# Reordering the first batch of an attention + bilinear feed-forward kernel: transposes of a pair next to that pair's products, more dummy products, and a later identity

## Chip, cores, metric

The kernel runs on one core of a Trainium2 chip. The metric is the time of one execution in device microseconds.

In the text "dummies" are matrix products of zeros whose result nobody reads. They keep TensorE busy. The "granted clock" is the share of its full speed that TensorE had, as the profiler recorded it.

## The reference

```python
# attention part, per batch and head (8 x 8 heads, 576 tokens, head size 64)
kv  = einsum('bhsd,bhse->bhde', k, v)        # no softmax: 64x64 per head
out = einsum('bhsd,bhde->bhse', q, kv)
x   = out / sqrt(mean(out*out, -1) + 1e-6) * g_norm
# heads side by side: x is 4608 tokens x 512
# feed-forward: d_ff 1536
y   = ((x @ w_a) * (x @ w_b)) @ w_out
```

## The kernel before

TensorE does the work of the feed-forward strip by strip (9 strips of 512 tokens) and puts the attention of later batches between. Only the first batch has nothing to hide behind. It is done in four pairs of heads. For each pair:

- `early_qT(p)`: 12 transposes of q on TensorE, then one copy on VectorE out of PSUM, the memory that TensorE writes to.
- `early_kv(p)`: 12 small products k.T v, then two copies into a block-diagonal tile (ScalarE, then VectorE).
- `xu(p, h)`: x = q kv for half h of the tokens, and its square on ScalarE.
- `ss(p, h)`: sums of squares by a product with ones; then `norm`: reciprocal root on ScalarE, scaling on VectorE into `xt`, the input of the feed-forward.

Pair 0 is loaded in float32 by the hardware queues and cast on the engines. Pairs 1 to 3 are loaded with a cast by Pool's software queue, nine loads of 144 KB, and the weights follow in the same queue.

```python
for n, src, eng in (("q", q, nc.scalar), ("k", k, nc.sync), ("v", v, nc.sync)):
    ...                                        # raw loads of pair 0
ident = const.tile([128, 128], BF16)
make_identity(nc, ident)                       # on Pool, ahead of Pool's loads
for p in range(1, NP):                         # NP = 4
    early_load(early[0], 0, slice(2 * p, 2 * p + 2))   # q, k, v of pair p
# ... cut: weights, batch 1
dummies(10)
# ... casts of pair 0
at0.early_qT(0, fpsum)
at0.early_kv(0, fpsum)
dummies(3)
at0.xu(0, 0)
at0.xu(0, 1)
at0.early_qT(1, fpsum)
for p in range(1, NP):
    if p + 1 < NP:
        at0.early_qT(p + 1, fpsum)             # pair p+1 ahead of the products of pair p
    dummies(3)
    last = p == NP - 1
    at0.early_kv(p, fpsum, act=last)
    at0.ss(p - 1, 0, fpsum)
    if last:
        dummies(2)
    at0.xu(p, 0)
    # ... cut: ss(p - 1, 1), xu(p, 1)
# ... cut: last sums, then the feed-forward of strip 0 begins
```

Of the kernel before, what the change touches and what calls it, by code (L numbers as in the profile page):

```python
# [15 lines left out]
def kernel(  # L16
# [19 lines left out]
    NP = H // 2  # L36
# [21 lines left out]
    fpsum = ctx.enter_context(tc.tile_pool(name="fpsum", bufs=4, space=bass.MemoryType.PSUM))  # L58
# [20 lines left out]
    def early_tiles(b):  # L79
        t = {n: shared(n, H, EC)[0:EP] for n in ("k", "v")}  # L80
        t["q"] = first.tile([EP, H, EC, D], BF16, name=f"eq{b}")
        return t

    def early_load(t, b, hs):
        for n, src in (("q", q), ("k", k), ("v", v)):
            nc.gpsimd.dma_start(  # L86
                out=t[n][:, hs, :, :],
                in_=src[b, hs].rearrange("h (sp c) d -> sp h c d", c=EC),
            )

    early = [early_tiles(0), early_tiles(1)]
# [3 lines left out]
    for n, src, eng in (("q", q, nc.scalar), ("k", k, nc.sync), ("v", v, nc.sync)):  # L95
        raw[n] = first.tile([EP, 2, EC, D], FP32, name=f"raw_{n}")
        eng.dma_start(out=raw[n], in_=src[0, h0].rearrange("h (sp c) d -> sp h c d", c=EC))
    ident = const.tile([128, 128], BF16)
    make_identity(nc, ident)
    for p in range(1, NP):  # L100
        early_load(early[0], 0, slice(2 * p, 2 * p + 2))


# [71 lines left out]
    def dummies(n):  # L175
        if n:
            ps = apsum.tile([128, 512], FP32, name="w_ps", tag="at")
            for _ in range(n):
                nc.tensor.matmul(ps, lhsT=zt[:, 0:128], rhs=zt, start=True, stop=True)  # L179
# [210 lines left out]
    at0 = Attn(0, early[0])  # L390
# [3 lines left out]
    def lead(u, *kcs, pools=(None, None)):  # L394
        for kc in kcs:
            for which, pool in zip("ab", pools):
                us[u].mm(which, kc, pool)
# [9 lines left out]
    dummies(3)  # L407
    at0.xu(0, 0)
    at0.xu(0, 1)
    at0.early_qT(1, fpsum)  # L410
    for p in range(1, NP):
        if p + 1 < NP:
            at0.early_qT(p + 1, fpsum)
        dummies(3)
        last = p == NP - 1
        at0.early_kv(p, fpsum, act=last)
        at0.ss(p - 1, 0, fpsum)
        if last:
            dummies(2)
        at0.xu(p, 0)  # L420
        if not last:
            at0.ss(p - 1, 1, fpsum)
            at0.xu(p, 1)
    p = NP - 1
    at0.ss(p - 1, 1, fpsum, split=True)
    s21 = at0.s_ps
    at0.xu(p, 1)
    dummies(1)
    at0.ss(p, 0, fpsum)
    at0.norm(p - 1, 1, s21)  # L430
    at0.ss(p, 1, fpsum)
    lead(0, 0, 1, 2, pools=(fpsum, apsum))
    lead(1, 0, 1, 2)
    lead(0, 3)
# [103 lines left out]
```

## Time and profile before

| | before |
|---|---|
| median of the first three runs | 336.59 us |
| profiled execution | 336.12 us, span 334.2 us |
| TensorE busy | 97% of the span |
| first feed-forward product that needs xt of pair 2 | 24.70 us |

The page of the kernel before gives busy time by engine, and the granted TensorE clock in tenths of full speed in 40 slices of 8.36 us:

```profile
span 334.2 us, 4562 instructions
...
PE 324.5 (97%) x1761; PEld 155.2 (46%) x1761; DVE 131.0 (39%) x225; ACT 133.9 (40%) x280; POOL 62.2 (19%) x78
...
PEclk9769999999999999999999999999999999999999
```

TensorE is the bound. What can be gained is at the start, where it is busy with dummies or waits, and where the second and third slices show a clock of 0.7 and 0.6.

The timeline of TensorE before (start us, duration us, engine, line, what; in brackets the idle time ahead of it and what ended it):

```profile
8.18 0.56 PE L215 MATMUL q_ps<-ident,eq_91 96*64 96x96 bf16 x12
11.17 0.56 PE L215 MATMUL q_ps<-ident,eq_91 96*64 96x96 bf16 x12 [2.43 <-DMA eq_91<-in_q_dram]
11.66 0.82 PE L179 MATMUL w_ps<-zt 128*128 128x512 bf16 x3
12.41 0.67 PE L200 MATMUL kv_ps<-v_t,k_t 96*64 96x64 bf16 x12
...
15.26 1.46 PE L179 MATMUL w_ps<-zt 128*128 128x512 bf16 x3
16.65 0.66 PE L200 MATMUL kv_ps<-v_t,k_t 96*64 96x64 bf16 x12
...
20.18 0.66 PE L200 MATMUL kv_ps<-v_t,k_t 96*64 96x64 bf16 x12
...
24.70 0.38 PE L314 MATMUL a_ps<-xt_160,wa_t 128*128 128x512 bf16 x1 [0.23 <-DVE xt_160 L267]
```

The transposes at 8.18 are those of pair 1, those at 11.17 of pair 2. TensorE takes its products in the order of the program, so kv of pair 1 at 12.41 also waited for q of pair 2. By the semaphores of the trace all of pair 1 had landed at 10.39. Note the three dummies: 0.82 us at 11.66, but 1.46 us at 15.26.

The same stretch by windows (window, its length, busy time of each engine with instructions, PEclk, DMA share, GB/s):

```profile
8.96:12.37 3.41, 1.20 (x15) 0.64 (x15) 0.73 (x2) 0.00 (x0) 2.47 (x4) 1.00 1.31 199
12.37:22.61 10.24, 9.79 (x70) 4.65 (x70) 3.42 (x8) 4.75 (x14) 8.50 (x12) 0.50 1.54 190
```

In the first window TensorE was busy for 1.20 of 3.41 us. In the 10.24 us after it, it had half the clock, although it was busy.

One trap of these views: they count the time ahead of the first clock record (5.55 us in this profile) as full speed. The ten dummies at the start take 4.45 us, twice what ten take later (0.22 us from one to the next).

### The profile page before, as it was taken

The page shows a single profiled execution, that of the slowest core. Times are in us where ns is not written, and L with a number is a line of the kernel's source. Part 1 is how long each engine was busy: PE and PEld are TensorE (multiplying, and loading weights), DVE is VectorE, ACT ScalarE, POOL GpSimd, SP SyncE. Part 2 cuts the span into 40 slices and gives each one's busy share as a digit, 9 for nine tenths or more (in the row PEclk, how much of TensorE's full clock was granted, in tenths as well). Part 3 has the DMA queues.
Part 4 walks back from the last instruction along what each step waited for, and adds up shares of the span by engine and source line. Part 5 has one row for each costly group of instructions (what it writes and reads, how often), then busy time and mean ns, then how long its engine had stood idle before and what let it go on. Part 6 is the DMA issues. An engine that isn't in the chain of part 4 may idle for free.

```text
span 334.2 us, 4562 instructions
## 1 busy us (share of the span) xinstructions
PE 324.5 (97%) x1761; PEld 155.2 (46%) x1761; DVE 131.0 (39%) x225; ACT 133.9 (40%) x280; POOL 62.2 (19%) x78
## 2 busy tenths in 40 slices
PE   7699999999999999999999999999999999999995
PEld 3344454545544454444444454445444444444442
DVE  3334354455344433443345334524452333232311
ACT  3253364366355335632463336423553222323210
POOL 8865700703400610061004300000000000000000
PEclk9769999999999999999999999999999999999999
DMA  7999999995973793289215960410001010000022
GB/s 158 190 195 199 204 184 168 185 167 66 161 110 56 100 187 67 63 106 173 69 25 88 183 114 17 88 64 2 31 33 32 38 59 32 31 33 31 31 65 94
DMA packets 80230, 32.60 MB, mean 98 GB/s; under 512 B 51920, under 2 KB 75728, under 8 KB 80208
## 3 DMA queue, kind: packets, MB, share of 16 engines
q0 software_dynamic: 59888, 18.44, 50.9%
q1 hardware_dynamic: 19968, 13.44, 15.8%
q10 hardware_dynamic: 352, 0.43, 0.4%
q8 instruction: 14, 0.23, 0.3%
q14 instruction: 8, 0.07, 0.1%
HBM read 37.75 MB, written 12.98 MB: 152 GB/s over the span
## 4 chain that ended last, share of the span: by engine, by line
PE 94%; DMA 2%; ACT 1%; POOL 1%; DVE 1%; issue 0%; POOLq 0%; ACTq 0%
PE a_ps L314 28%; PE o_ps L342 28%; PE b_ps L314 28%; PE x_ps L243 3%; PE s_ps L258 3%; DMA eq_91<-in_q_dram 2%; PE kv_ps L231 2%; PE w_ps L179 1%; PE kv_ps L200 1%; PE q_ps L215 1%; ACT rs L265 1%; POOL eq_91 L86 0%; POOL k_t L86 0%; ACT qs_667 L221 0%; POOL v_t L86 0%
## 5 line engine op out<-in xcount | busy, mean ns | idle before, releaser
L326 DVE TENSOR_TENSOR abt<-b_ps,a_sb 128x512 bf16<-128x512 f32 x108 | 74.6, 692 | 119.1 <-PE b_ps L314 119.1
L324 ACT CAST a_sb<-a_ps 128x512 bf16<-128x512 f32 x108 | 63.1, 586 | 90.2 <-PE a_ps L314 88.4
L342 PE MATMUL o_ps<-wo_t,abt 128*128 128x512 bf16 x432 | 98.6, 379 | 0.0
L314 PEld LDWEIGHTS <-wb_t 128*128 128x128 bf16 x432 | 42.3, 98 | 51.3 <-issue 0.5
L342 PEld LDWEIGHTS <-abt 128*128 128x128 bf16 x432 | 42.3, 98 | 48.7 <-issue 0.5
L314 PEld LDWEIGHTS <-wa_t 128*128 128x128 bf16 x432 | 41.6, 98 | 43.1 <-DMA wa_t<-in_moe_w_a_dram 0.4
L314 PE MATMUL a_ps<-xt_160,wa_t 128*128 128x512 bf16 x108 | 40.9, 379 | 0.2 <-DVE xt_160 L267 0.2
L314 PE MATMUL a_ps<-xt_158,wa_t 128*128 128x512 bf16 x108 | 41.0, 380 | 0.0
L314 PE MATMUL a_ps<-xt_159,wa_t 128*128 128x512 bf16 x108 | 40.9, 379 | 0.0
L314 PE MATMUL b_ps<-xt_159,wb_t 128*128 128x512 bf16 x108 | 40.9, 379 | 0.0
L314 PE MATMUL a_ps<-xt_161,wa_t 128*128 128x512 bf16 x108 | 40.9, 379 | 0.0
L314 PE MATMUL b_ps<-xt_161,wb_t 128*128 128x512 bf16 x108 | 40.9, 379 | 0.0
L314 PE MATMUL b_ps<-xt_158,wb_t 128*128 128x512 bf16 x108 | 40.9, 379 | 0.0
L314 PE MATMUL b_ps<-xt_160,wb_t 128*128 128x512 bf16 x108 | 40.9, 379 | 0.0
L251 ACT ACTIVATE sq<-x_ps 128x288 bf16<-128x288 f32 x64 | 26.1, 410 | 29.7 <-PE x_ps L243 29.4
L265 ACT ACTIVATE rs<-s_ps,eps_t 128x288 f32<-128x288 f32 x64 | 31.5, 497 | 5.4 <-PE s_ps L258 4.9
L367 ACT COPY o_sb<-o_ps 128x512 f32<-128x512 f32 x17 | 9.9, 585 | 43.6 <-PE o_ps L342 43.6
L369 DVE COPY o_sb<-o_ps 128x512 f32<-128x512 f32 x18 | 12.4, 692 | 35.5 <-PE o_ps L342 35.5
L161 POOL COPY gate_t<-qT 1x1 bf16<-1x1 bf16 x5 | 0.9, 176 | 111.0 <-DMA qT<-scr 111.0
L148 POOL DMA_DIRECT2D scr<-in_q_dram x12 | 19.6, 1636 | 3.1 <-issue 2.4
L258 PE MATMUL s_ps<-sq,ones 128*128 128x288 bf16 x64 | 19.0, 300 | 0.6 <-ACT rs L265 0.4
L267 DVE SCALAR_TENSOR_TENSOR xt_160<-x_ps,g_col,rs 128x288 bf16<-128x288 f32 x16 | 8.3, 517 | 19.6 <-ACT rs L265 19.6
(76 smaller groups left out, 166.7 us busy)
## 6 DMA issues: line engine op xcount, KB each, us to landing
out_dram<-o_sb SPq DMA_DIRECT2D x23, 256.0 KB, 2.0
scr<-in_q_dram POOLq DMA_DIRECT2D x12, 288.0 KB, 6.7
k_t<-in_k_dram POOLq DMA_DIRECT2D x6, 512.0 KB, 8.7
v_t<-in_v_dram POOLq DMA_DIRECT2D x6, 512.0 KB, 10.8
out_dram<-o_sb SPq DMA_DIRECT2D x13, 128.0 KB, 2.4
wo_t<-in_moe_w_out_dram POOLq DMA_DIRECT2D x2, 768.0 KB, 14.8
wa_t<-in_moe_w_a_dram POOLq DMA_DIRECT2D x5, 256.0 KB, 8.6
wb_t<-in_moe_w_b_dram POOLq DMA_DIRECT2D x5, 256.0 KB, 9.2
```

Source lines behind the costliest of these rows:

```text
L148: nc.gpsimd.dma_start(out=scr[:, :, hl, :].rearrange("p s d -> s p d"), in_=qv[hl])
L243: nc.tensor.matmul(ps, lhsT=self.kvd[:, p, :], rhs=self.q[p][:, h * HF : (h + 1) * HF], start=True, stop=True,)
L251: nc.scalar.activation(sq, ps, AF.Square)
L258: nc.tensor.matmul(ps, lhsT=ones, rhs=self.sq[p, h], start=True, stop=True)
L265: nc.scalar.activation(rs, ps, AF.Abs_reciprocal_sqrt, bias=eps_t)
L267: nc.vector.scalar_tensor_tensor(out=xt[p][:, t0 : t0 + HF], in0=self.x_ps[p, h], scalar=g_col, in1=rs, op0=ALU.mult, op1=ALU.mult,)
L314: nc.tensor.matmul(getattr(self, which), lhsT=w[:, kc, self.fc * 128 : (self.fc + 1) * 128], rhs=xt[kc][:, t0 : t0 + STRIP], start=(kc == ...
L324: nc.scalar.copy(a_sb, self.a)
L326: nc.vector.tensor_mul(t, self.b, a_sb)
L342: nc.tensor.matmul(o_ps[s, g], lhsT=ab[s, fc][:, g * 128 : (g + 1) * 128], rhs=wo_t[:, fc, :], start=(fc == 0), stop=(fc == FC - 1),)
L367: nc.scalar.copy(o_sb, ps)
L369: nc.vector.tensor_copy(o_sb, ps)
```

## The change

The intent: let the transposes of a pair go directly ahead of that pair's own products, so that pair 1 doesn't wait for the loads of pair 2; fill the waits for loads with more dummies (6, 4, 4 for 3, 3, 3); and issue pair 1's loads ahead of the identity on Pool.

```diff
+    early_load(early[0], 0, slice(2, 4))
     ident = const.tile([128, 128], BF16)
     make_identity(nc, ident)
-    for p in range(1, NP):
+    for p in range(2, NP):
         early_load(early[0], 0, slice(2 * p, 2 * p + 2))
# ... cut
     at0.xu(0, 1)
-    at0.early_qT(1, fpsum)
+    last = NP - 1
     for p in range(1, NP):
-        if p + 1 < NP:
-            at0.early_qT(p + 1, fpsum)
-        dummies(3)
-        last = p == NP - 1
-        at0.early_kv(p, fpsum, act=last)
+        at0.early_qT(p, fpsum)
+        dummies(6 if p == 1 else 4)
+        at0.early_kv(p, fpsum, act=p == last)
         at0.ss(p - 1, 0, fpsum)
# ... cut: the rest of the loop is written differently, its order is the same
```

More of the change, by code (lines that the diff above doesn't have):

```diff
@@ L409 @@
     at0.xu(0, 1)
-    at0.early_qT(1, fpsum)
+    last = NP - 1
     for p in range(1, NP):
-        if p + 1 < NP:
-            at0.early_qT(p + 1, fpsum)
-        dummies(3)
-        last = p == NP - 1
-        at0.early_kv(p, fpsum, act=last)
+        at0.early_qT(p, fpsum)
+        dummies(6 if p == 1 else 4)
+        at0.early_kv(p, fpsum, act=p == last)
         at0.ss(p - 1, 0, fpsum)
-        if last:
+        if p == last:
             dummies(2)
         at0.xu(p, 0)
-        if not last:
-            at0.ss(p - 1, 1, fpsum)
-            at0.xu(p, 1)
-    p = NP - 1
-    at0.ss(p - 1, 1, fpsum, split=True)
-    s21 = at0.s_ps
-    at0.xu(p, 1)
+        at0.ss(p - 1, 1, fpsum, split=p == last)
+        at0.xu(p, 1)
+    s_ps = at0.s_ps
     dummies(1)
-    at0.ss(p, 0, fpsum)
-    at0.norm(p - 1, 1, s21)
-    at0.ss(p, 1, fpsum)
+    at0.ss(last, 0, fpsum)
+    at0.norm(last - 1, 1, s_ps)
+    at0.ss(last, 1, fpsum)
     lead(0, 0, 1, 2, pools=(fpsum, apsum))
```

## The prediction

> **What bounds it.** TensorE: the page gives PE 97% of the span, and the timeline shows it almost without gaps from 24.70 us, when the first feed-forward product on xt2 starts. The change touches only what is before, so its worth is how much earlier that point comes.
>
> The start, from the timeline and the semaphore times of the loads:
> - TensorE's order puts the transposes of pair 2 ahead of the products of pair 1. Pair 1 has landed at 10.39 (last is v), but TensorE waits idle from 8.74 to 11.17 for the q of pair 2 (the chain of waits: 7.6 us of that load), and kv of pair 1 runs only at 12.48.
> - The granted clock falls to 0.50 at 12.37 and stays there until 22.61, 10.24 us. The Trainium skill, "TensorE: Matmul & The Clock Gate", Part 1, puts the decision in free-running windows of 3413 ns; the trace agrees (10.24 = 3 x 3.413), and the window before the fall, 8.96 to 12.37, holds the idle 2.4 us. Under it a dummy product takes 0.43-0.48 us instead of 0.21.
> - Loads are a queue at about 0.7 us per 144 KB: q, k, v of pair 2 land at 11.12, 11.81, 12.55, of pair 3 at 13.35, 14.07, 14.77; the first four weight pieces at 15.5-17.7.
>
> **What changes.** Pool's identity (about 0.75 us ahead of the first load) moves behind pair 1's three loads; these are issued 0.75 us earlier, the later ones not. They then overlap the raw loads of pair 0, which may land 0-0.4 us later; I expect v of pair 1 at 9.7-10.3. Each pair becomes: transposes, dummies (6, then 4, 4), kv, sums and x. Five dummies more, 1.1 us warm, but they fill waits.
>
> **Sum (estimates from these durations, warm clock).** Transposes of pair 1 end at 8.8, six dummies at 10.1, kv of pair 1 at 10.2 (was 12.48). Copies 0.5 us, x: 11.3-11.7. Transposes of pair 2 to 12.3, dummies to 13.2, kv of pair 2 at 13.2 (was 16.72), x to 14.7; transposes 15.3, dummies 16.2, kv of pair 3 at 16.2 (was 20.2). The tail on ScalarE and VectorE (squares, reciprocal roots, xt2) 3.8 us, where it was 4.5: first xt2 product at about 20.0 instead of 24.70, 4.7 us earlier.
>
> **What of it lasts.** Weights land in time (piece for block 2 at 20.45, wanted at 22.5), batch 1's loads and wo too (43.65 against 46.0). Tightest is batch 2: its last v lands at 58.94, wanted at 64.4 now and 59.7 after; and the first three output writes (768 KB) would now run among those loads, not after them. I take off 0.3 us on average, up to 1.5.
>
> **Prediction:** 336.59 - 4.4 = 332.2 us, range 330.6 to 334.6; faster by over 2% 0.04, within 2% 0.94, slower 0.02.
>
> **Shows it right:** clock 1.0 from about 5.5 us to the end; no wait of TensorE for pair 2's q; kv of pair 1 at 10-10.6; first xt2 product at 19.5-20.5; everything from there shifted equally.
>
> **Shows it wrong:** clock still falling (the same page, Part 4, says transposes do not count as busy in the same way, so a window of transposes and small products may still count as idle): then about 2 us gained only. Raw loads of pair 0 late by over 0.5 us. TensorE waiting at batch 2's kv around 60 us for loads delayed by output writes: gain given back there.

## The result

The changed kernel took 332.63 us (median of four: 331.58, 331.84, 333.42, 333.50), before 336.60 (four runs, 336.28 to 336.74). The ratio is 0.988, 95% interval 0.984 to 0.992: clear of noise, and under 2%. Ratios here are the mean time of one kernel's fast runs over that of the other's in the same rounds, so not quite the ratio of the medians.

Two groups can be seen in the four times, about 1.8 us apart. They are called the slow and the quick group here. The first profile fell into the upper group (333.42 us). The same kernel was run again later, and that profile fell into the lower (331.44 us). Both are shown, since at the start they differ in one main thing, the time at which the clock rose.

The page of the second profile of the changed kernel:

```profile
span 329.5 us, 4572 instructions
...
PE 321.4 (98%) x1766; PEld 154.0 (47%) x1766; DVE 130.8 (40%) x225; ACT 134.1 (41%) x280; POOL 62.6 (19%) x78
...
PEclk9999999999999999999999999999999999999999
```

Its TensorE timeline, to be held against that of before:

```profile
8.13 0.56 PE L216 MATMUL q_ps<-ident,eq 96*64 96x96 bf16 x12
8.62 1.47 PE L180 MATMUL w_ps<-zt 128*128 128x512 bf16 x6
10.02 0.47 PE L201 MATMUL kv_ps<-v_t,k_t 96*64 96x64 bf16 x12
...
12.98 0.47 PE L201 MATMUL kv_ps<-v_t,k_t 96*64 96x64 bf16 x12
...
15.93 0.47 PE L201 MATMUL kv_ps<-v_t,k_t 96*64 96x64 bf16 x12
...
17.99 0.38 PE L180 MATMUL w_ps<-zt 128*128 128x512 bf16 x1 [0.54 <-DVE xt L268]
...
20.05 0.38 PE L315 MATMUL a_ps<-xt,wa_t 128*128 128x512 bf16 x1 [0.58 <-DVE xt L268]
```

No product waits for a load any more, and kv of the three pairs comes at 10.02, 12.98 and 15.93 instead of 12.41, 16.65 and 20.18. The first product on xt of pair 2 comes at 20.05 instead of 24.70: 4.65 us earlier. The span is 4.7 us shorter (334.2 - 329.5), so nothing was given back in this execution.

The windows that were shown of before:

```profile
8.96:12.37 3.41, 3.08 (x36) 1.59 (x34) 1.12 (x4) 1.70 (x5) 3.35 (x5) 1.00 1.31 200
12.37:22.61 10.24, 8.79 (x73) 4.21 (x71) 4.24 (x10) 5.17 (x15) 7.74 (x11) 1.00 1.55 191
```

TensorE is busy for 3.08 us of the first window, and the clock does not fall.

The first profile of the changed kernel, TensorE's timeline:

```profile
6.21 0.86 PE L216 MATMUL q_ps<-ident,eq 96*64 96x96 bf16 x12 [0.57 <-DVE eq L403]
...
7.41 1.46 PE L180 MATMUL w_ps<-zt 128*128 128x512 bf16 x3
...
10.08 1.70 PE L180 MATMUL w_ps<-zt 128*128 128x512 bf16 x6
11.71 0.47 PE L201 MATMUL kv_ps<-v_t,k_t 96*64 96x64 bf16 x12
...
21.74 0.38 PE L315 MATMUL a_ps<-xt,wa_t 128*128 128x512 bf16 x1 [0.58 <-DVE xt L268]
```

The three dummies at 7.41 take 1.46 us, the time of half the clock. Here the clock records begin at full speed only at 10.58 us; in the profile of before at 5.55, in the second one of the changed kernel at 5.84. Both start cold, at half speed, and this execution became warm 4.7 us later than the other. Neither the page nor the mean clock of an execution shows that: the mean is 1.0 for both. From there both go alike, 1.7 us apart (21.74 against 20.05), which is the distance of the two groups.

The clock records lie on a grid of 3.41 us (they last, for example, 6.83, 10.24 or 324.27 us, which is 2, 3 and 95 times 3.413) that has no fixed place against the start of the kernel. The Trainium skill, "TensorE: Matmul & The Clock Gate", Part 1, says so: the window "doesn't reset when your kernel starts". The two profiles agree. The window grid of the first puts a window at 3.76 to 7.17, into which the end of the ten dummies, 0.57 us of idle time and the first transposes fell; it did not raise the clock. The grid of the second puts one at 2.43 to 5.84, which is dummies to 94%; it did. In the other twelve profiles of this text the clock rose between 3.83 and 6.98 us. That the grid decides is argued from these profiles; no run set the grid.

### The profile page after: what moved, and what is told of

It is laid out like the page before. It is cut to its first block, busy times and chain, and to the rows that moved or that the text cites. A ratio compares the mean times of both kernels' runs of the same rounds, so it can differ in the third digit from the quotient of the medians.

```text
span 331.4 us, 4572 instructions
## 1 busy us (share of the span) xinstructions
PE 323.2 (98%) x1766; PEld 155.0 (47%) x1766; DVE 132.1 (40%) x225; ACT 133.8 (40%) x280; POOL 62.5 (19%) x78
## 3 DMA queue, kind: packets, MB, share of 16 engines
HBM read 37.75 MB, written 12.98 MB: 153 GB/s over the span
## 4 chain that ended last, share of the span: by engine, by line
PE 94%; DVE 2%; DMA 1%; ACT 1%; issue 0%; ACTq 0%; DVEq 0%
PE o_ps L343 28%; PE a_ps L315 28%; PE b_ps L315 28%; PE x_ps L244 2%; PE s_ps L259 2%; PE kv_ps L232 2%; PE w_ps L180 2%; DMA raw_q<-in_q_dram 1%; PE q_ps L216 1%; PE kv_ps L201 1%; ACT rs L266 1%; DVE xt L268 0%; DVE kr_t L187 0%; DVE eq L403 0%; DVE abt L327 0%
## 5 line engine op out<-in xcount | busy, mean ns | idle before, releaser
L315 PE MATMUL a_ps<-xt,wa_t 128*128 128x512 bf16 x432 | 112.0, 380 | 0.6 <-DVE xt L268 0.6
L315 PE MATMUL b_ps<-xt,wb_t 128*128 128x512 bf16 x432 | 111.9, 379 | 0.0
L268 DVE SCALAR_TENSOR_TENSOR xt<-x_ps,g_col,rs 128x288 bf16<-128x288 f32 x64 | 32.8, 517 | 30.6 <-ACT rs L266 30.5
L259 PE MATMUL s_ps<-sq,ones 128*128 128x288 bf16 x64 | 18.0, 287 | 0.4 <-ACT rs L266 0.4
L244 PE MATMUL x_ps<-qT,kvd 128*128 128x288 bf16 x48 | 13.8, 286 | 0.0
L180 PE MATMUL w_ps<-zt 128*128 128x512 bf16 x30 | 10.7, 498 | 1.7 <-DVE eps_t L108 1.2
L244 PEld LDWEIGHTS <-kvd 128*128 128x128 bf16 x64 | 6.3, 99 | 8.4 <-DVE kvd L210 1.3
L259 PEld LDWEIGHTS <-ones 128*128 128x128 bf16 x64 | 6.3, 98 | 7.2 <-issue 0.7
L232 PE MATMUL kv_ps<-v_t,kr_t 128*128 128x128 bf16 (+1 forms) x120 | 8.4, 219 | 0.1
L232 PEld LDWEIGHTS <-kr_t 128*128 128x128 bf16 (+1 forms) x120 | 7.2, 97 | 2.2 <-DVE kr_t L184 1.3
```

The costliest lines, as they stand in the source:

```text
L180: nc.tensor.matmul(ps, lhsT=zt[:, 0:128], rhs=zt, start=True, stop=True)
L232: nc.tensor.matmul(ps[:, p, :], lhsT=self.k[0:r, c, hs, :], rhs=self.v[0:r, hs, c, :], start=(c == 0 and p == 0), stop=(c == NCH and p == ...
L244: nc.tensor.matmul(ps, lhsT=self.kvd[:, p, :], rhs=self.q[p][:, h * HF : (h + 1) * HF], start=True, stop=True,)
L259: nc.tensor.matmul(ps, lhsT=ones, rhs=self.sq[p, h], start=True, stop=True)
L268: nc.vector.scalar_tensor_tensor(out=xt[p][:, t0 : t0 + HF], in0=self.x_ps[p, h], scalar=g_col, in1=rs, op0=ALU.mult, op1=ALU.mult,)
L315: nc.tensor.matmul(getattr(self, which), lhsT=w[:, kc, self.fc * 128 : (self.fc + 1) * 128], rhs=xt[kc][:, t0 : t0 + STRIP], start=(kc == ...
```

## Experiments

All outputs are right. Each run of five rounds gave six times of its kernel, and eleven of before, which are shared by runs of one call. The first of the three calls ran on another chip than the other two, so ratios to before in the same rounds are the fair comparison between calls. The mean granted clock is listed for each execution, and it sorts them by falls of the clock, though not by late rises: a clock of 0.995 is one window of 3.41 us at half speed (half of 3.41 over 333), 0.985 is three. Values of 0.997 to 0.999 need no such window: trim's profile, at 0.997, has half speed only in its last 1.7 us.

Of the 33 times of before, 10 lie between 332.2 and 333.3 us, all at a clock of 0.998 or more. The other 23 lie between 334.7 and 337.4, all at 0.995 or less. So before has two forms as well, and by their times (336.28 to 336.74) the first four runs happened to be all of the slower form.

### after_again: the changed kernel once more

No edit.

> The changed kernel once more, for more of its executions. Its four times lay in two groups, 331.6-331.8 and 333.4-333.5 us, and its profile (333.4) shows the clock at full speed only from 10.58 us, where before's shows it from 5.55. Theory: the clock is decided in free-running windows of 3.41 us, so it depends on where the kernel starts in a window whether the ten dummies at the start fill one; then the times here again form two groups about 1.8 us apart (331.6 and 333.4), and the profile shows whichever of the two starts goes with its time. Rival: the spread is that of the loads; then times spread evenly, and the landing times, not the clock, differ from the first profile.

Measured: 331.37, 331.38, 331.43, 331.44, 331.73 and 333.33 us; before in the same rounds 332.4 to 337.3 without the slow one, ratio 0.990 (0.986 to 0.995). The two groups stand as the theory said, and the profile, of the lower group, has the early clock. The landing times in the two profiles do not differ in a way that would explain it: the last load of pair 1 landed at 9.36 us in the slow profile and at 9.46 in the quick one. The rival falls.

### ident_only: before with the identity moved alone

```diff
+    early_load(early[0], 0, slice(2, 4))
     ident = const.tile([128, 128], BF16)
     make_identity(nc, ident)
-    for p in range(1, NP):
+    for p in range(2, NP):
```

> Before, with only the identity moved behind pair 1's three loads. Loads should land 1.0 us earlier as in the changed kernel (last of pair 1 at 9.4, q of pair 2 at 10.1), but TensorE still waits for q of pair 2, from 8.7 to 10.1. Theory (the order is the cause, through the idle wait and the clock that falls after it): the clock still falls and most of the gain is missing, 335.0-336 us. Rival (earlier loads are the cause): 332-333.5 us.

Measured: 332.37, 332.39, 332.71, 332.79 at a clock of 1.0, and 336.02, 336.15 at 0.985 and 0.982; ratio 0.997 (0.990 to 1.003). Neither expectation was met as written: the median fits the rival and the mean neither. TensorE's timeline of its profile, which is of the quick form:

```profile
8.18 0.56 PE L216 MATMUL q_ps<-ident,eq 96*64 96x96 bf16 x12
10.26 0.56 PE L216 MATMUL q_ps<-ident,eq 96*64 96x96 bf16 x12 [1.52 <-DMA eq<-in_q_dram]
```

It has the same order of products as before, and the wait for q of pair 2 is still there, but it is 1.52 us and the clock did not fall, although the window from 6.52 to 9.94 us was busy to only 63%. So the old order does not always make the clock fall. Its cost without a fall is small: 332.6 us is the mean of these four and of before's ten quick executions alike.

### order_only: the new order alone

```diff
# changed kernel with
-    early_load(early[0], 0, slice(2, 4))
     ident = const.tile([128, 128], BF16)
     make_identity(nc, ident)
-    for p in range(2, NP):
+    for p in range(1, NP):
# ... cut
-        dummies(6 if p == 1 else 4)
+        dummies(3)
```

> The new order of transposes alone: identity first as before, three dummies a pair as before. Theory (order and clock): kv of pair 1 at 10.4 us when its v has landed, idle 1 us only, clock does not fall, first xt2 product near 20.5, 331.5-333 us. Rival (the extra dummies hold the clock): the clock falls again at about 12 and the time is 334-336 us.

Measured: 330.68, 330.76, 331.23, 331.31, 331.39 at a clock of 1.0 and 333.23 at 0.995; ratio 0.989 (0.984 to 0.994). The lines of its profile that correspond to those of the changed kernel:

```profile
9.53 0.44 PE L200 MATMUL kv_ps<-v_t,k_t 96*64 96x64 bf16 x12 [0.19 <-DMA v_t<-in_v_dram]
...
19.10 0.38 PE L314 MATMUL a_ps<-xt,wa_t 128*128 128x512 bf16 x1 [0.58 <-DVE xt L267]
```

The order alone carries the whole gain. Five times are below the expected 331.5 to 333, since v of pair 1 landed at 9.49 us and not at 10.4; four of its six times are even below the best of the changed kernel's repetition, by up to 0.7 us. Its first product on xt of pair 2 comes at 19.10 us against 20.05, which is near the five dummies less (1.1 us at 0.22 us each). The one execution at 0.995 shows that a fall of one window remains possible.

### no_ident: the changed kernel with the identity back in front

```diff
-    early_load(early[0], 0, slice(2, 4))
     ident = const.tile([128, 128], BF16)
     make_identity(nc, ident)
-    for p in range(2, NP):
+    for p in range(1, NP):
```

> The changed kernel with the identity back in front of the loads (order and dummies only). Theory: six dummies end at about 10.1 in a run with an early warm clock and v of pair 1 lands at 10.4, so it loses 0.3 us at most, 331.8-332.2 in the quick group and no loss in the slow group (333.4). Rival (the earlier loads carry a good part of the gain): 1 us slower than the changed kernel in both groups.

Measured: 331.65, 331.83, 331.87, 331.92, 332.89, 333.40; ratio 0.991 (0.987 to 0.996). The four quick ones are 0.35 us above the five quick ones of the changed kernel (means 331.82 and 331.47), so the theory's 0.3 us and not the rival's 1 us. In its profile kv of pair 1 comes at 10.40 against 10.02, because the cast of v of pair 0 came late (its raw load landed at 6.39 against 6.13), not because of Pool's loads: v of pair 1 landed at 9.46 in both. That raw load landed at 6.03 to 6.18 us in the other four profiles with the identity in front, so its delay is not shown to come from the identity's place.

### before_filled: before, with the wait filled

```diff
     at0.early_qT(1, fpsum)
+    dummies(7)
```

> Before, order and identity as they were, with seven more dummies after the transposes of pair 1, that is in the wait for q of pair 2 (1.5 us warm). It does not shorten the wait, it only keeps TensorE busy in it. Theory (the wait costs by letting the clock fall, and only some of before's executions, those at 332.4-332.9, are spared): the clock falls in none, all times at 332.3-333.3 and, where the opening dummies miss their window, about 334. Rival (the wait itself is the cost): 335-337 in most executions as before.

Measured: 333.08, 333.25, 333.34, 333.41, 333.60, 334.50, all at a clock of 0.998 or more, while 7 of the 11 executions of before in the same rounds had 0.995 or less. Ratio 0.996 (0.990 to 1.002), so the mean alone would not tell; the clocks do, since no execution fell. The filling has a price: the mean is 333.53 us, 0.9 us above before's four executions of these rounds that did not fall (332.66), and three times are up to 0.3 us above the expected 333.3. TensorE's timeline shows what was bought (one of the seven records is missing):

```profile
8.99 0.56 PE L215 MATMUL q_ps<-ident,eq 96*64 96x96 bf16 x12 [0.79 <-DMA eq<-in_q_dram]
9.49 1.69 PE L179 MATMUL w_ps<-zt 128*128 128x512 bf16 x6
11.10 0.56 PE L215 MATMUL q_ps<-ident,eq 96*64 96x96 bf16 x12
```

The loads were late in this execution (v of pair 1 at 10.34 us, q of pair 2 at 11.05), kv of pair 1 came at 12.34 as in the profile of before, and yet the first product on xt of pair 2 came at 21.77 instead of 24.70, and this execution took 333.60 us and not 336. The same wait, spent busy, costs about 2.5 us less. That separates the wait from the clock that falls after it.

### no_dummies: the new order without dummies ahead of the products

```diff
-        dummies(6 if p == 1 else 4)
+        dummies(0)
```

> The changed kernel with no dummies ahead of the products of pairs 1 to 3 (6, 4, 4 taken out). Theory (with the new order the loads are there in time and the dummies are pure work in the chain): kv of pair 3 about 2 us earlier, limited by its v landing near 13.9 us; 329.8-330.8 where the clock is warm early. Rival (they hold the clock): the clock falls in some executions and those are at 333 us or more; the mean is slower than the changed kernel.

Measured: 329.63, 329.89, 330.01, 330.05, 330.40, 330.44; median 330.03, ratio 0.986 (0.980 to 0.991). It is 1.7 us below the mean of the changed kernel's repetition (330.07 against 331.78; another call, so the two ratios to before, 0.986 and 0.990, are the fairer comparison). Of the same call is open12, the changed kernel with two more dummies at the start: its best time is 331.47, a microsecond above the worst here. Part of the rival is true: three executions had a clock of 0.990 or 0.993, so it does fall now and then. But those took 330.01, 330.05 and 330.44, as quick as the rest. Here the dummies held the clock at a higher price than its fall. Why a fall cost nothing here is open, since no such execution was profiled; in late_nolast below, the two executions at 0.995 are 1.4 us above the other four.

TensorE's timeline at the start, and at batch 2's kv:

```profile
9.48 0.44 PE L201 MATMUL kv_ps<-v_t,k_t 96*64 96x64 bf16 x12 [0.67 <-DMA v_t<-in_v_dram]
...
11.66 0.44 PE L201 MATMUL kv_ps<-v_t,k_t 96*64 96x64 bf16 x12 [0.15 <-DMA v_t<-in_v_dram]
...
13.97 0.44 PE L201 MATMUL kv_ps<-v_t,k_t 96*64 96x64 bf16 x12
...
59.06 0.38 PE L232 MATMUL kv_ps<-v_t,kr_t 64*128 64x128 bf16 x4 [0.21 <-DMA v_t<-in_v_dram]
```

Now the products follow the loads: kv of pair 1 waits for its v, that of pair 2 for 0.15 us, that of pair 3 hardly. In the changed kernel six dummies end at 10.0 and v had landed at 9.46; four dummies before kv of pair 2 and again of pair 3 stood in front of data that were there. And at 59.06 a new limit shows: the last v of batch 2.

### open12: twelve dummies at the start

```diff
-    dummies(10)
+    dummies(12)
```

> The changed kernel with twelve dummies at the start in place of ten, so that TensorE is busy through the 0.3-0.6 us that it waits for the first cast. Theory (the slow group, 333.3-333.5, is where the opening dummies leave a window not full enough): the slow group is gone or rarer, all at 331.3-331.9. Rival (the window is lost by the transposes, which do not count): the slow group stays, 1 in 3.

Measured: 331.47 to 332.05, six of six; ratio 0.991 (0.986 to 0.996). No execution in the slow group, where 3 of 10 of the changed kernel's were. With so few this points to the theory without showing it (with three in ten slow, six quick ones in a row come about once in eight). Its profile fits: a window from 3.56 to 6.98 us, 0.2 us off that of the changed kernel's slow profile, was full, and the clock rose at its end. But in before_filled a window from 3.49 to 6.91 us raised the clock with ten dummies. The mean is not lower than that of the repetition, 331.76 against 331.78: the quick ones lost 0.3 us.

### lean: a candidate

```diff
-    dummies(10)
+    dummies(12)
# ... cut
-        dummies(6 if p == 1 else 4)
+        dummies(3 if p == 1 else 0)
# ... cut
-    dummies(1)
     at0.ss(last, 0, fpsum)
```

> A candidate: the changed kernel with 12 dummies at the start, 3, 0, 0 ahead of the products of pairs 1 to 3, and without the single dummy ahead of the last sums, which waited 0.53 us for a PSUM buffer in the profile and held the sums back. Expected: first xt2 product at about 17.7 us instead of 20.05; batch 2's kv then wants its v, which lands at 58.9, at 57.5, so up to 1.4 us come back there; 329.5-331 us.

Measured: 329.56 to 331.16, median 330.29, ratio 0.986 (0.981 to 0.992): the median is in the range, but no better than no_dummies. The profiled execution (330.67 us) came to xt of pair 2 at 19.28 and not 17.7. The clock fell for one window, and v of pair 1 landed only at 10.01 us, for which TensorE waited 0.38 us. By windows:

```profile
9.95:13.37 3.42, 2.37 (x41) 1.47 (x40) 1.85 (x5) 2.48 (x7) 3.38 (x6) 1.00 1.37 195
13.37:16.78 3.41, 3.15 (x31) 2.03 (x33) 1.73 (x4) 2.05 (x7) 3.41 (x5) 0.50 1.71 185
```

The window ahead of the fall was busy to 69% (2.37 of 3.42), and the longest idle gap in it was 0.55 us.

### before_again: the kernel before, one more profile

No edit.

> The kernel before, for one more profile and one more time. In its first profile v of pair 1 landed at 10.39 us, in all later profiles, of whatever kernel with whatever place of the identity, at 9.4-10.0. Theory: that is the spread of executions and the identity's place does not set it; then here it lands at 9.4-10.1 too. The time is 332.4-333.4 with a clock that does not fall, or 334.8-337.4 with one that does; the profile shows which goes with the time.

Measured: 336.54 us, clock 0.983, full speed from 5.53 to 12.36 us and half for 10.24 us, with TensorE idle for 2.41 us ahead of the transposes of pair 2: the first profile over again. Here v of pair 1 landed at 10.27 us. The expectation (9.4 to 10.1) was missed, and its ground was wrong: before_filled's profile, taken earlier, had 10.34. The v of pair 1 landed at 10.27 to 10.39 in the three profiles that have before's order and the identity in front, at 9.46 and 9.49 in the two with the new order and the identity in front, and at 9.36 to 10.01 in the nine with the identity moved. The order of TensorE's products is hardly the reason: it differs only from 8.5 us on, and k of pair 1 had landed at 8.66 and 8.69 us in the two with the new order, against 9.47 to 9.59 in the three. Whether the place of the identity makes late loads rarer stays open; the figures allow it.

### late_kv: batch 2's attention one slot later

```diff
# no_dummies with
-        s_at = 1 if s == 1 else 0
+        s_at = 2 if s == 1 else 0
```

> no_dummies with batch 2's attention begun one slot (8 products, 1.7 us) later in strip 1. In no_dummies TensorE waited for batch 2's last v, which lands near 59.0 us in every profile whatever came before. Theory (the start's gain is given back at that load): the wait of about 1.2 us goes, the time is 328.6-329.2. Rival (something else holds it at 330): 329.7-330.4 as before.

Measured: 330.83 to 331.87, median 331.57; ratio 0.990 (0.985 to 0.995). Slower than no_dummies, which neither theory allowed for. The wait at batch 2's kv is gone, but there is another one at the end of the strip, which no_dummies does not have, where the feed-forward wants what this attention makes:

```profile
81.16 0.38 PE L315 MATMUL a_ps<-xt,wa_t 128*128 128x512 bf16 x1 [0.86 <-DVE xt L268]
```

The wait had cost little: between the first output product and batch 3's kv the profile of no_dummies lost 0.44 us against the repetition of the changed kernel (38.99 against 38.55 us). The 0.86 us are more than that. The profiled execution also had a clock that fell at 7.25 us for a window.

### late_nolast: late_kv without the single dummy at the end

```diff
-    dummies(1)
     at0.ss(last, 0, fpsum)
```

> late_kv without the single dummy ahead of the last sums. That dummy waits about 0.5 us for a PSUM buffer and the last sums wait behind it. Theory: 0.3-0.5 us less than late_kv, 328.2-328.8. Rival (ScalarE's chain of squares and roots ends the stage anyway): no difference.

Measured: 330.17, 330.38, 330.47, 330.72, and 331.47, 332.26 at a clock of 0.995; ratio 0.988 (0.983 to 0.993). The means differ by 0.5 us from late_kv in the expected direction (330.91 against 331.42), with overlapping intervals; the level expected was wrong, as late_kv's was.

### trim: late_nolast with twelve opening dummies and one in each wait for kv's copies

```diff
-    dummies(10)
+    dummies(12)
# ... cut
-        if p == last:
-            dummies(2)
+        dummies(2 if p == last else 1)
```

> late_nolast with 12 dummies at the start, and one dummy put where TensorE waits for the copies of kv in pairs 1 and 2. These should cost nothing (they fill a wait of 0.33 us) and make a fall or a late rise of the clock rarer: same best time as late_nolast, 328.2-328.8, and no slow execution. If they cost, 0.2-0.6 us more.

Measured: 330.24 to 330.81, median 330.40, ratio 0.987 (0.982 to 0.992), no execution below a clock of 0.997. No slow execution, and with open12 the smallest spread (0.6 us); the level is above the expected 328.2 to 328.8 and near late_nolast's best, and it carries the same 0.86 us at the strip's end. The combination that these runs suggest, trim with batch 2's attention in its old slot, was not run.

## Why the prediction was right, and where it was not

- **Total.** Predicted 332.2 us (330.6 to 334.6), measured 332.63. The saving at the first product on xt of pair 2 was predicted at 4.7 us and is 4.65 us in the profile of the quick form (24.70 to 20.05), but 2.96 us in the first profile (21.74), whose kv of pair 1, at 11.71, is outside the forecast too. That the total fits to 0.4 us owes something to luck: two of the four executions lay in the slow group, and all four of before were of its slower form. In after_again the ratio is 0.990, a gain of about 3.3 us and not of 4.4.
- **The old order waits for q of pair 2 and lets the clock fall.** Right, and shown in two ways: the new order alone (order_only) gains everything, and filling the wait (before_filled) keeps the clock without shortening the wait. What the prediction did not see is that the fall is not certain. 10 of 33 executions of before escape it, and then the changed kernel gains only about 1.1 us (means 332.55 and 331.47). The 4 us of the first comparison are mostly the clock's, and happened to be measured against four executions whose times all lie among those that fell (a clock is on record for the profiled one alone, 0.983).
- **"Clock 1.0 from about 5.5 us".** Wrong for part of the executions. The prediction took the early rise from before's profile as given. By the profiles it depends on where the grid of windows lies, and 3 of the 10 executions of the changed kernel lie in the group that is 1.8 us slower; the one of them that was profiled rose late, and the mean clock can't tell for the others. Two of the first four were in that group; that is the 0.4 us between 332.2 and 332.63, and more.
- **The identity.** Predicted: loads issued 0.75 us earlier, v of pair 1 at 9.7 to 10.3. The first load is issued at 1.29 us instead of 1.49, so 0.2 us earlier: Pool stood idle for 0.84 us ahead of it, which the profile puts down to Pool's own sequencer. The first packet of this queue moved at 4.70 us after and 4.78 before, so the earlier issue bought nothing there. v landed at 9.36, but it did so too with the identity in front (9.46 in no_ident). The step was worth at most 0.35 us (no_ident), and in the one profile of no_ident that came by way of pair 0.
- **"Five dummies more ... but they fill waits."** Wrong. With loads as early as 9.4 us they fill no wait for pairs 2 and 3. Taking all of them out gives 330.03 us.
- **Batch 2.** 0.3 us was taken off for output writes among its loads. Its last v landed at 58.99 us in the first profile, against 58.94 before, and at 58.78 in the second; the writes did not delay it. That term was zero in the quick execution. In the first profile a copy of 64x512 on VectorE took 1.36 us there (0.28 in the second) and the products after it ended about 0.2 us late; why it took so long was not tested.

## What to carry to other kernels

When a change at the start of a kernel moves the time by some microseconds, look at the granted clock of every execution, not of one profile: here the kernel before has two forms and so has the kernel after, and medians of four can be of either. An in-order engine should not have the next stage's load ahead of this stage's work; if a wait can't be avoided, filling it can keep the clock, at a price (0.9 us in before_filled). But dummies are paid for as soon as the data come earlier than they end: try the version without them each time the order changes (here 330.03 us against 331.4 to 332.6).

## What the Trainium skill lacked or had wrong

- "TensorE: Matmul & The Clock Gate", "Why this matters for your kernels" and "HAM oscillation": the advice is to leave no idle gap over about 3 us, or one idle window. The clock fell after a window that was 35% busy and held most of a gap of 2.43 us (before), and in lean after one that was 69% busy with no gap over 0.55 us. So the length of a gap alone does not decide; the page's "A second HAM failure mode" does tell of short idle times that let the clock oscillate. No single limit on the busy share of the window before fits either: 71% was followed by a fall in late_nolast and by none in no_dummies, and 63% by none in ident_only.
- The same page, Part 1, the table of the two states: that one busy window raises the clock. In before a window busy to 93% (15.8 to 19.2 us, at half clock; the profile models the ends of products) did not raise it, and one busy to 77% did in late_kv. The page's caution that the start varies from run to run is right; its remark that the penalty is under 1% holds here for the distance between a late and an early rise (1.8 of 332 us), which is still half of what this change is worth.
- The same page, Part 4: that transposes do not count as busy in the same way. These runs do not settle it: the first profile's window of 3.76 to 7.17 us was busy to 83%, to 64% without its transposes, and did not raise the clock, but windows busy to 69% without transposes both did (before_filled) and did not (open12).
- "DMA: Bandwidth & Descriptors", Specifications: about 1 us to the first byte of a load issued from Pool. At the start of this kernel the first packet of that queue moved at 4.64 to 4.84 us, after an issue that began at 1.3 or 1.5 us, so 3.2 us or more later, in all fourteen profiles; the hardware queues began at 1.8 us after an issue at 0.74. The raw loads of pair 0 were moving meanwhile, so how much of it is the queue's own delay was not tested.
